# v loaded and cast three pairs later than q and k, the last pieces of w_out moved behind pair 16's casts, and one spread product per unit one step later

## The chip, the cores and the metric

The kernel runs on one core of a Trainium2 chip. The metric is the device time of one execution in microseconds (us); a kernel is run several times and its median is taken. Before the change the median is 483.12 us over 3 runs (481.99 to 483.59).

The engines are TensorE (PE; its weight loads are listed as PEld), VectorE (DVE), ScalarE (ACT), GpSimd (POOL) and SyncE (SP), which here only issues DMAs. Each engine works through its own list of instructions in order and waits on semaphores for the others.

## The reference

```python
# q, k, v: (8, 12, 448, 64); x: (3584, 768), w_in: (768, 2048), w_out: (2048, 768)
scores = scale * np.matmul(q, k.transpose(0, 1, 3, 2))
m = np.max(scores, axis=-1, keepdims=True)
e = np.exp(scores - m)
attn = e / (np.sum(e, axis=-1, keepdims=True) + np.exp(-m) + 1e-09)
attn_out = np.matmul(attn, v)
x = attn_out.transpose(0, 2, 1, 3).reshape(B * S, H * D)
h = x @ w_in
g = h * np.tanh(np.log1p(np.exp(h)))
out = g @ w_out
```

So it is an attention over 8 batches of 12 heads, whose denominator has one extra term, and behind it two dense layers with a Mish between them.

## The kernel before

**Pairs, steps and units.** Two heads make a *pair*: 48 pairs, 6 to a batch. A pair has 4 *steps*, each with up to two blocks of 128 rows of scores. The first 6 pairs are the *head*, a loop of its own (L616). Behind it come *units* of 3 pairs, 12 steps each, n = 0 to 11 (L651, counter u; unit u scores pairs 3u to 3u + 2, so unit 2 has pairs 6 to 8 and unit 4 pairs 12 to 14). Scores are computed three steps ahead of the step whose exponentials run (`scores_ahead`).

**What a step does.** `exps` (ScalarE) takes the exponentials of a step's scores from a PSUM tile `sc` into `en`. `flush_late` then emits the evacuations that earlier steps left in the list `late`. `scores` (TensorE) computes the scores of step n + 3, and VectorE takes their negated maximum (`negm`, L330). Because each engine works in order, the order of these calls is the order on each engine.

**From en to the value product.** `en` has to be transposed to `eT`. Mostly SP issues a DMA transpose for it (`normalise`, L420); pairs 5, 6 and 7 (`BY_PE`) are turned on TensorE in four quarters j (`turn_on_pe`, L432), each followed by an evacuation on VectorE (L435). `av_pair` (L460) multiplies `eT` with `v_bf`; the result goes into `xT` (L475, or L473). For pairs 0 to 11 the division by the denominator is done at this point: `spread_rden` multiplies (TensorE, L391) the reciprocals, split into a high and a low part (`hl`), with an identity, so that each row's reciprocal stands in every row of a PSUM tile, and ScalarE or VectorE copies it to `rb` (L400). From pair 12 on VectorE multiplies `en` itself before the transpose (L412, seven instructions a pair).

**The mo tiles.** There are two PSUM tiles `mo`, handed out by `mo_take` and given back when the evacuation is emitted. The turns, the spreads, the transposes of q and k in the head and in step 4 of unit 2 (`late_tp`), the dummy products that keep TensorE busy (L270) and the two dense layers all use them. When `spread_rden` is called in units 2 and 3, its copy goes to `slow`: it is emitted two steps later on ScalarE, behind that step's exponentials.

**The end of a unit.** After the 12 steps each unit from u = 2 on computes 8 blocks of the first dense layer for a batch (`mm1_mish`, L496, Mish on ScalarE in L502), with the transposes of q and k of the next unit's pairs (L206, evacuated in L242 to L260) and the first scores of the next unit between them. The second dense layer (L549) fills the steps of units from 4 on.

**Loads and casts.** SP's queue, in order, carries the loads of q, k and v (`load_pair`, L128), the DMA transposes and the stores. `ld_pool` has three buffers for each of q, k and v. GpSimd casts q, k and v to bf16 (L179, L180, L186). In the head, pair p + 5 is loaded and pair p + 3 cast in pair p's turn; in a unit, at n = 0, 3 and 6 (`LOAD_AT`), pairs are loaded 4 ahead and cast 3 ahead (`LEAD`). The value product of a pair comes three pairs behind its scores.

**Weights.** GpSimd also issues the DMAs of w_in (12 pieces) and w_out (8 pieces), L162, at the steps in `W_AT`. Where `W_BEHIND` (or the call itself) names a pair, GpSimd first copies two elements of that pair's `eT` (`marks`, L157): it waits there until that transpose has landed. The first four pieces of w_out are the left half of its columns, which unit 4 reads; the last four are the right half, which unit 5 reads first.

Of the kernel before, what the change touches and what calls it, by code (L numbers as in the profile page):

```python
# [19 lines left out]
def kernel(  # L20
# [27 lines left out]
    N_PAIRS = B * HP  # L48
# [59 lines left out]
    def flush_late():  # L108
        while late:
            late.popleft()()  # L110
# [10 lines left out]
    def load_pair(p, names="qkv"):  # L121
        if p >= N_PAIRS:
            return
        b, h0 = p // HP, (p % HP) * 2
        for nm in names:
            src = dict(q=q, k=k, v=v)[nm]
            t = ld_pool.tile([SP_, 2, NT * D], FP32, tag=f"{nm}_f", name=f"{nm}_f")
            nc.sync.dma_start(  # L128
                out=t, in_=src[b, h0 : h0 + 2].rearrange("h (p t) d -> p h (t d)", t=NT)
            )  # L130
            loaded.setdefault(p, {})[nm] = t
# [33 lines left out]
    def cast_pair(p, with_v=True):  # L165
        if p >= N_PAIRS:
            return
        q_f, k_f, v_f = (loaded[p].get(nm) for nm in "qkv")
        q_bf = bf_pool.tile([SP_, NT, 2, D], BF16, tag="q_bf", name="q_bf")
        k_bf = bf_pool.tile([SP_, NT, 2, D], BF16, tag="k_bf", name="k_bf")  # L170
        v_bf = bf_pool.tile([SP_, 2, NT * D], BF16, tag="v_bf", name="v_bf", bufs=12)
        by_t = "p h (t d) -> p t h d"
        q_t, k_t = (t.rearrange(by_t, t=NT) for t in (q_f, k_f))
        if p == 0:
            nc.vector.tensor_copy(out=k_bf, in_=k_t)
            for half in (slice(0, NT // 2), slice(NT // 2, NT)):
                nc.vector.tensor_copy(out=q_bf[:, half], in_=q_t[:, half])
        else:
            nc.gpsimd.tensor_copy(out=q_bf, in_=q_t)  # L179
            nc.gpsimd.tensor_copy(out=k_bf, in_=k_t)  # L180
        casted[p] = (q_bf, k_bf, v_bf)
        if with_v:
            cast_v(p)

    def cast_v(p):
        nc.gpsimd.tensor_copy(out=casted[p][2], in_=loaded.pop(p)["v"])  # L186

    def transpose_pair(p, bank=None):
# [93 lines left out]
    def scores_ahead(limit):  # L282

        while rg["next"] < limit and rg["used"] < len(sc_tiles):
            rg["used"] += 1
            scores(rg["next"])
            rg["next"] += 1
# [301 lines left out]
    LEAD = UNIT_PAIRS + 1  # L589
    LOAD_AT = (0, 3, 6)  # L590
    HEAD = HP

    BY_PE = {HEAD - 1: 1, HEAD: -2, HEAD + 1: 2}
    AV_AT = {0: {1: 3, 5: 4, 8: 5}, 1: {1: 8, 4: 6, 8: 7}}
    RDEN_AT = {0: {0: 3, 2: 4, 6: 5}, 1: {0: 8, 2: 6, 6: 7}, 2: {3: 10, 5: 11}}

    W_AT = ({0: 4, 5: 1}, {1: 2, 3: 1, 5: 1, 7: 1, 9: 1}, {1: 1, 3: 1, 5: 1, 7: 1})
    W_BEHIND = {(0, 0): HEAD - 2, (2, 1): HEAD + 4}
    for p, names in (0, "kq"), (1, "qk"), (0, "v"), (2, "qk"), (1, "v"), (2, "v"):
        load_pair(p, names)  # L600
    keep_busy(8, bank=sc_tiles[0][:, 0, :])
# [14 lines left out]
    for p in range(HEAD):  # L616
        for s in range(STEPS):
            exps(p * STEPS + s)
            if s == 0 and p == 0:
                evac_qk(1, act=True)  # L620
            flush_late()
            if s == 1:
                late.extend(held)
                held.clear()
                flush_late()
            if s == 2:
                evac_qk(p + 2, act=p % 2 == 0)
            scores_ahead(HEAD * STEPS + 3)
            if s == 0:
                transpose_pair(p + 2)  # L630
                if p:
                    denominators(p - 1)
            if s == 1 and p:
                turn_on_pe(p - 1, NT - 1)
            if s == 3 and p == 1:
                load_w(2)
            if s == 2:
                if p >= 3:
                    spread_rden(p - 3)
                cast_pair(p + 3)  # L640
            if s == 3:
                if p >= 3:
                    av_pair(p - 3, hold=True)
                if p + 5 < 10:
                    load_pair(p + 5)
                normalise(p, dma=p not in BY_PE)
            if s < 3:
                keep_busy(2, half=p)
    denominators(HEAD - 1)

    for u in range(UNITS_PER_B, N_UNITS + 2 * UNITS_PER_B):  # L651
        attn = u < N_UNITS
        filler = deque()
        for part in plan.get(u, []):
            filler.extend(mm2_part(*part))
        total, done, acc = sum(w for _, w in filler), 0, 0.0
        p0 = u * UNIT_PAIRS
        if attn and u >= first_mm2:
            av_with.update({p0 + i: p0 + i - UNIT_PAIRS for i in range(UNIT_PAIRS)})
        end = min((u + 1) * UNIT_PAIRS, N_PAIRS) * STEPS  # L660

        for n in range(steps):
            pi, s = divmod(n, STEPS)
            p, idx = p0 + pi, p0 * STEPS + n
            late_tp = u == UNITS_PER_B and n == STEPS
            exps(idx)
            if u == UNITS_PER_B + 1 and n == 0:
                for j in range(2):
                    turn_on_pe(HEAD, j, busy_first=3)
            flush_late()  # L670
            if late_tp:
                transpose_pair(p0 + 2)
                evac_qk(p0 + 2)
            if held and n == 1:
                late.extend(held)
                held.clear()
                flush_late()
            late.extend(slow)
            slow.clear()
            acc += weight[n]  # L680
            want = int(total * acc / sum(weight) + 1e-6)
            while done < want:
                fn, w = filler.popleft()
                fn()
                done += w
            scores_ahead(end)
            if n in LOAD_AT:
                load_pair(p0 + LOAD_AT.index(n) + LEAD)
                cast_pair(p0 + LOAD_AT.index(n) + LEAD - 1)
            for pe, n0 in BY_PE.items():  # L690
                j = n - n0
                first = 2 if pe == HEAD else 0
                if pe // UNIT_PAIRS == u - 1 < first_mm2 - 1 and first <= j < NT:
                    turn_on_pe(pe, j, busy_first=1)
            spread = RDEN_AT.get(u - UNITS_PER_B, {})
            if n in spread:
                on_act = u < first_mm2
                spread_rden(
                    spread[n], copy=nc.scalar.copy if on_act else nc.vector.tensor_copy,
                    behind=slow if on_act else late,  # L700
                )
            early = AV_AT.get(u - UNITS_PER_B)
            if early is not None and n == 7:
                keep_busy(6, bank=mo_free[0])
            if early is not None:
                if n in early:
                    av_pair(early[n], half=p)
            elif s == (2 if pi else 0) and N_PAIRS <= p < N_PAIRS + UNIT_PAIRS:
                av_pair(p - UNIT_PAIRS)
            if u - UNITS_PER_B < len(W_AT):  # L710
                at = (u - UNITS_PER_B, n)
                load_w(W_AT[at[0]].get(n, 0), behind=W_BEHIND.get(at))
        assert done == total

        moe = u < N_UNITS + UNITS_PER_B
        b, w = (u - UNITS_PER_B) // UNITS_PER_B, u % UNITS_PER_B
        nxt = p0 + UNIT_PAIRS
        todo = sorted(range(p0, nxt), key=lambda p: p in BY_PE)
        for f in range(FF_U):
            if moe:  # L720
                mm1_mish(b, w * FF_U + f)
            if u == UNITS_PER_B and f == 3:
                load_w(3, behind=p0 + 2)
            if not attn:
                continue
            if f == 0:
                denominators(p0, UNIT_PAIRS)
                for p in todo if p0 < LATE_DIV else todo[:1]:
                    normalise(p, dma=p not in BY_PE)
            if f == 5 and u == UNITS_PER_B + 1:  # L730
                spread_rden(p0, copy=nc.scalar.copy)
            if f == 4:
                scores_ahead(min(nxt * STEPS + 1, N_PAIRS * STEPS))
            if f in (1, 3, 5):
                transpose_pair(nxt + f // 2, bank=f // 2 % 2)
                evac_qk(nxt + f // 2)
            if f >= FF_U - 2:
                scores_ahead(min(nxt * STEPS + f - FF_U + 4, N_PAIRS * STEPS))
            if f in (3, FF_U - 1) and p0 >= LATE_DIV:
                p = todo[1 + f // (FF_U - 1)]  # L740
                normalise(p, dma=p not in BY_PE)
# [32 lines left out]
```

## Time and profile before

| | before |
|---|---|
| median of 3 runs | 483.12 us |
| the profiled execution | 483.9 us |
| its span, first to last instruction | 482.0 us |
| VectorE busy | 360.3 us (75%) |
| ScalarE busy | 345.3 us (72%) |
| GpSimd busy | 104.3 us (22%) |

How to read the profile: a row of the timeline has start and duration in us, the engine, the line of the kernel, the operation, what it writes and reads (out<-in), how many instructions are merged (x), and in brackets the idle time of the engine before it and what ended it. A row of waits has who waited for whom, the total in us, how often, and the longest. DMAs are issued by SPq and POOL; the time until one lands is told separately. A row of a stretch of time has its bounds, its length, the busy time of each engine with the number of instructions, the granted TensorE clock, the DMA share and GB/s.

### The profile page before, as it was taken

What the parts mean: (1) busy time and instruction counts of PE and PEld (TensorE: products, weight loads), DVE (VectorE), ACT (ScalarE), POOL (GpSimd) and SP (SyncE); (2) the same over time, 40 slices, a digit from 0 to 9 for tenths busy, and PEclk for the clock granted to TensorE, in tenths of its full rate; (3) what the DMA queues carried; (4) which work ended last, traced back from release to release, by engine and by line L of the source; (5) the groups of instructions that cost most, each with busy time, mean ns of one, the idle gap of its engine ahead of it and who ended that gap; (6) DMA issues with size and microseconds to landing.
All of it is one profiled execution on the core that took longest, in us unless ns stands there. A gap on an engine that the chain in (4) does not pass through costs nothing.

```text
span 482.0 us, 9366 instructions
## 1 busy us (share of the span) xinstructions
PE 460.2 (95%) x3291; PEld 257.7 (53%) x3291; DVE 360.3 (75%) x715; ACT 345.3 (72%) x907; POOL 104.3 (22%) x187
## 2 busy tenths in 40 slices
PE   7788899999899999999999999999999999999996
PEld 2344445545555555556555565555555565556563
DVE  5989748669899888889898998888898879421021
ACT  5998868888687869788797968787887978312300
POOL 4633618106022220404040311204040200000000
PEclk9989999999999999999999999999999999999999
DMA  8999999999999979998999999989979695961122
GB/s 238 228 207 220 239 204 216 160 197 248 211 251 228 250 157 211 229 182 224 201 251 164 256 164 219 220 193 227 194 222 197 160 175 121 154 141 34 34 66 67
DMA packets 204976, 91.10 MB, mean 189 GB/s; under 512 B 161792, under 2 KB 201472, under 8 KB 204928
## 3 DMA queue, kind: packets, MB, share of 16 engines
q1 hardware_dynamic: 197408, 84.18, 81.1%
q0 software_dynamic: 7488, 6.29, 9.0%
q8 instruction: 26, 0.43, 0.4%
q14 instruction: 22, 0.18, 0.1%
q10 hardware_dynamic: 32, 0.02, 0.0%
HBM read 45.61 MB, written 11.01 MB: 117 GB/s over the span
## 4 chain that ended last, share of the span: by engine, by line
PE 65%; DVE 7%; ACT 6%; DMA 6%; issue 1%; SPq 0%; DVEq 0%
PE mo L549 23%; PE mo L496 22%; PE sc L309 7%; ACT en L343 6%; PE sc L460 5%; DMA eT<-en 5%; DVE negm L330 4%; PE sc L496 3%; PE sc L206 3%; DVE en L412 1%; DVE xT L473 1%; PE mo L460 1%; DVE o_sb L532 0%; DMA out_dram<-o_sb 0%; DVE qd L252 0%
## 5 line engine op out<-in xcount | busy, mean ns | idle before, releaser
L343 ACT ACTIVATE en<-sc,negm 128x448 bf16<-128x448 f32 x336 | 209.2, 644 | 22.3 <-DVE negm L330 20.6
L330 DVE TENSOR_REDUCE negm<-sc 128x2 f32<-128x896 f32 x192 | 182.8, 970 | 40.6 <-PE sc L309 30.1
L549 PE MATMUL mo<-w_out_sb,gT 128*128 128x384 bf16 (+1 forms) x1024 | 166.7, 306 | 0.4 <-DVE rb L400 0.4
L496 PE MATMUL mo<-xT,w_in_sb 128*128 128x448 bf16 x672 | 142.2, 352 | 1.3 <-DMA w_in_sb<-in_moe_w_in_dram 0.9
L549 PEld LDWEIGHTS <-gT 128*128 128x128 bf16 x1024 | 96.3, 98 | 56.0 <-issue 1.9
L502 ACT ACTIVATE gT<-mo 128x448 bf16<-128x448 f32 x112 | 59.5, 543 | 81.1 <-PE mo L496 80.9
L496 PEld LDWEIGHTS <-w_in_sb 128*128 128x128 bf16 x768 | 72.5, 98 | 65.0 <-issue 3.2
L412 DVE TENSOR_SCALAR en<-en,rden 128x448 bf16<-128x448 bf16 x252 | 74.7, 369 | 0.8
L179 POOL CAST q_bf<-q_f 112x512 bf16<-112x512 f32 x47 | 29.2, 622 | 211.7 <-DMA q_f<-in_q_dram 191.2
L309 PE MATMUL sc<-kT,qd 128*128 128x448 bf16 x252 | 71.6, 354 | 1.8 <-DVE qd L252 1.8
L343 ACT ACTIVATION_READ_ACCUMULATOR en<-sc,negm 128x1 f32 x336 | 72.1, 215 | 0.0
L532 DVE COPY o_sb<-mo 128x384 f32<-128x384 f32 (+1 forms) x64 | 31.9, 498 | 48.3 <-PE mo L549 48.1
L460 PE MATMUL sc<-eT,v_bf 112*64 112x448 bf16 x336 | 39.8, 357 | 1.7 <-DMA eT<-en 0.9
L309 PEld LDWEIGHTS <-qd 128*128 128x128 bf16 x252 | 24.5, 98 | 30.7 <-issue 12.9
L252 DVE TENSOR_SCALAR qd<-sc 64x448 bf16<-64x448 bf16 x72 | 27.8, 386 | 6.0 <-PE sc L206 5.2
L186 POOL CAST v_bf<-v_f 112x512 bf16<-112x512 f32 x48 | 30.0, 625 | 5.7 <-DMA v_f<-in_v_dram 5.4
L180 POOL CAST k_bf<-k_f 112x512 bf16<-112x512 f32 x47 | 29.3, 624 | 7.2 <-DMA k_f<-in_k_dram 5.9
L460 PEld LDWEIGHTS <-v_bf 112*64 112x64 bf16 x384 | 19.8, 109 | 20.5 <-issue 11.8
L260 ACT COPY kT<-sc 128x448 bf16<-128x448 bf16 x39 | 20.8, 533 | 0.6 <-PE sc L206 0.6
L496 PE MATMUL sc<-xT,w_in_sb 128*128 128x448 bf16 x96 | 20.8, 352 | 0.0
L473 DVE CAST xT<-sc 128x448 bf16<-128x448 f32 x33 | 20.3, 615 | 0.0
L206 PEld LDWEIGHTS <-q_bf 112*128 112x128 bf16 x192 | 13.5, 97 | 9.2 <-issue 1.0
(61 smaller groups left out, 281.2 us busy)
## 6 DMA issues: line engine op xcount, KB each, us to landing
k_f<-in_k_dram SPq DMA_DIRECT2D x48, 224.0 KB, 5.0
q_f<-in_q_dram SPq DMA_DIRECT2D x48, 224.0 KB, 4.8
v_f<-in_v_dram SPq DMA_DIRECT2D x48, 224.0 KB, 5.2
w_in_sb<-in_moe_w_in_dram POOLq DMA_DIRECT2D x12, 256.0 KB, 9.5
w_out_sb<-in_moe_w_out_dram POOLq DMA_DIRECT2D x8, 384.0 KB, 10.4
out_dram<-o_sb SPq DMA_DIRECT2D x7, 336.0 KB, 4.0
out_dram<-o_sb SPq DMA_DIRECT2D x8, 288.0 KB, 4.6
out_dram<-o_sb SPq DMA_DIRECT2D x8, 240.0 KB, 3.2
```

The lines of the kernel that those rows point to most:

```text
L179: nc.gpsimd.tensor_copy(out=q_bf, in_=q_t)
L180: nc.gpsimd.tensor_copy(out=k_bf, in_=k_t)
L186: nc.gpsimd.tensor_copy(out=casted[p][2], in_=loaded.pop(p)["v"])
L309: nc.tensor.matmul(sc[:, bk, 0:S], lhsT=qT[:, i].rearrange("d h r -> d (h r)"), rhs=kT, start=True, stop=True,)
L330: half_max[p] = nc.vector.tensor_reduce(out=negm, in_=sc[:, 0 : len(cols), 0:S], axis=AX.X, op=ALU.max, negate=True)
L343: e = nc.scalar.activation(out=st["en"][:, :, c, 0:SP_], in_=sc[:, bk, 0:S].rearrange("q (j c) -> q j c", j=NT), func=AF.Exp, bias=st["neg ...
L412: nc.vector.tensor_scalar(out=en[:, :, i, 0:SP_], in0=en[:, :, i, 0:SP_], scalar1=st["rden"][:, i : i + 1], scalar2=None, op0=ALU.mult,)
L460: mm = nc.tensor.matmul(av[h * 64 : (h + 1) * 64, 0:S], lhsT=v_bf[:, h, j * D : (j + 1) * D], rhs=e_h, start=(j == 0), stop=(j == NT - 1),)
L496: nc.tensor.matmul(h_ps[:, 0:S], lhsT=w_in_sb[:, dm, ff * 128 : (ff + 1) * 128], rhs=xT[b][:, dm, :], start=(dm == 0), stop=(dm == DM_T - 1),)
L502: nc.scalar.activation(out=gT[:, ff, b % 2 * S : b % 2 * S + S], in_=h_ps[:, 0:S], func=AF.Mish)
L532: nc.vector.tensor_copy(out=o_sb[:, cols.start : cols.start + n_dve], in_=st["o"][:, 0:n_dve])
L549: nc.tensor.matmul(st["o"][:, 0:n_cols], lhsT=gT[:, ff, i * 128 : (i + 1) * 128], rhs=w_out_sb[:, ff, cols], start=(ff == 0), stop=(ff == ...
```

## The change

Three things move.

- **v.** In the head, v is loaded for pairs up to 6 and cast for pairs up to 5 only. In a unit, at n = 0, 3 and 6, q and k are loaded 4 pairs ahead and cast 3 pairs ahead as before, v is loaded 1 pair ahead and cast for the pair of that very step. `cast_v` returns for pairs that don't exist.
- **w_out.** In unit 4 the pieces at steps 1, 3, 5 and 7 become pieces at steps 3, 5, 7 and 7, and the marker at step 1, which waited for the transpose of pair 10, goes. Step 3's piece comes behind the casts that step 3 issues, those of pair 16.
- **Spread.** In units 2 and 3, `spread_rden` of the middle one (pairs 4 and 6) is called at step 3 instead of step 2.

```diff
     def cast_v(p):
+        if p >= N_PAIRS:
+            return
         nc.gpsimd.tensor_copy(out=casted[p][2], in_=loaded.pop(p)["v"])
...
-    RDEN_AT = {0: {0: 3, 2: 4, 6: 5}, 1: {0: 8, 2: 6, 6: 7}, 2: {3: 10, 5: 11}}
-
-    W_AT = ({0: 4, 5: 1}, {1: 2, 3: 1, 5: 1, 7: 1, 9: 1}, {1: 1, 3: 1, 5: 1, 7: 1})
-    W_BEHIND = {(0, 0): HEAD - 2, (2, 1): HEAD + 4}
+    RDEN_AT = {0: {0: 3, 3: 4, 6: 5}, 1: {0: 8, 3: 6, 6: 7}, 2: {3: 10, 5: 11}}
+
+    W_AT = ({0: 4, 5: 1}, {1: 2, 3: 1, 5: 1, 7: 1, 9: 1}, {3: 1, 5: 1, 7: 2})
+    W_BEHIND = {(0, 0): HEAD - 2}
...
-                cast_pair(p + 3)
+                cast_pair(p + 3, with_v=p + 3 < HEAD)
...
-                    load_pair(p + 5)
+                    load_pair(p + 5, "qkv" if p + 5 <= HEAD else "qk")
...
-                load_pair(p0 + LOAD_AT.index(n) + LEAD)
-                cast_pair(p0 + LOAD_AT.index(n) + LEAD - 1)
+                at = p0 + LOAD_AT.index(n)
+                load_pair(at + LEAD, "qk")
+                load_pair(at + 1, "v")
+                cast_pair(at + LEAD - 1, with_v=False)
+                cast_v(at)
```

`RDEN_AT` and `W_AT` are indexed by unit - 2; in `RDEN_AT` a step maps to the pair whose reciprocals are spread there.

## The prediction

> **What bounds the kernel now.** I read the page first.
>
> ```profile
> span 482.0 us, 9366 instructions
> PE 460.2 (95%) x3291; PEld 257.7 (53%) x3291; DVE 360.3 (75%) x715; ACT 345.3 (72%) x907; POOL 104.3 (22%) x187
> PE   7788899999899999999999999999999999999996
> DMA  8999999999999979998999999989979695961122
> ```
>
> TensorE is busy 95% of the span, and it is below 9 tenths in the first slices (12 us each) only: whatever this change moves must show before about 125 us. So I asked who TensorE waits for, before and after 122 us, and where.
>
> ```profile
> PE mo L496 <- DMA w_in_sb<-in_moe_w_in_dram: 0.9, 1, 0.9
> PE sc L460 <- DMA eT<-en: 0.9, 1, 0.9
> PE sc L309 <- DVE qd L252: 1.8, 1, 1.8
> PE mo L496 <- DVE xT L473: 0.3, 1, 0.3
> ```
>
> The first two come from the waits up to 122 us, the last two are all there is behind it. So what is won or lost up to 122 us goes through to the end nearly whole. The timeline places the three.
>
> ```profile
> 58.48 1.69 PE L496 MATMUL mo<-xT,w_in_sb 128*128 128x448 bf16 x8 [0.92 <-DMA w_in_sb<-in_moe_w_in_dram]
> 101.31 0.95 PE L460 MATMUL sc<-eT,v_bf 112*64 112x448 bf16 x8 [0.86 <-DMA eT<-en]
> 122.05 0.55 PE L309 MATMUL sc<-kT,qd 128*128 128x448 bf16 x2 [1.75 <-DVE qd L252]
> ```
>
> They are the first w_in product (at the end of unit 2, whose twelve steps belong to pairs 6 to 8; the third piece of w_in is late), the value product of pair 9 (in unit 4, pairs 12 to 14; its transpose is late) and the first scores for unit 5, behind unit 4's normalisation. Together 3.53 us: that is the prize, and none of it is in the steady part.
>
> **v later.** Three v loads (pairs 7, 8, 9) and three v casts leave the head; they come back in the last attention units, where the DMA row has its first 6s and 5s in a row with 9s. TensorE's order of work is unchanged by this part. What does a load cost? At the start, with nothing else on the DMA engines, GpSimd's casts each begin on the landing of their tile; the first and the last of seven in a row:
>
> ```profile
> 8.70 0.62 POOL L179 CAST q_bf<-q_f 112x512 bf16<-112x512 f32 x1 [0.16 <-DMA q_f<-in_q_dram]
> 13.38 0.62 POOL L186 CAST v_bf<-v_f 112x512 bf16<-112x512 f32 x1 [0.17 <-DMA v_f<-in_v_dram]
> 30.00:101.00 71.00, 65.08 (x608) 35.61 (x606) 51.55 (x86) 57.82 (x155) 27.85 (x53) 1.00 1.16 205
> ```
>
> From 8.70 to 13.38 are six steps: 0.78 us a load, 2.3 us for three. The third row is a stretch of time; its last two numbers are the DMA share and GB/s. A share of 1.16 over 71 us is a backlog without a hole, so I take it that all later landings come 2.3 us earlier. The third w_in piece then lands near 56.1, pair 9's transpose near 99.0 instead of 101.3; both waits lose their cause (-0.92 and -0.86) as far as TensorE is not itself later. The three casts (1.9 us of GpSimd) were off the path. At the other end v of pairs 45 to 47 is cast a unit ahead of its product; with the free DMA there I put that at 0, and at 0.78 us a load if a store or a transpose were to wait behind one.
>
> **Spread product one step later.** TensorE does the same 16 small products, but the two PSUM banks `mo` change places. In unit 2, step 4 takes a bank for the transposes of pair 8. Before, that was the bank which the copy of spread 4 (ScalarE) had just freed. Now the spread is one step younger, holds its bank until step 5, and the transposes must take the bank of the third turn of pair 5, behind its evacuation; the fourth turn must then take the same bank again, behind the evacuations of q and k.
>
> ```profile
> 49.06 1.08 DVE L330 TENSOR_REDUCE negm<-sc 128x2 f32<-128x896 f32 x1
> 49.20 0.35 PE L270 MATMUL mo<-busy 128*128 128x448 bf16 x1 [0.41 <-DVE eT L435]
> 49.77 0.36 PE L206 MATMUL mo<-ident,q_bf 112*128 112x112 bf16 x4
> 50.06 0.61 DVE L435 COPY eT<-mo 112x896 bf16<-112x896 bf16 x1
> 50.59 0.38 DVE L242 TENSOR_SCALAR qd<-mo 128x448 bf16<-128x448 bf16 x1
> 51.19 0.61 DVE L330 TENSOR_REDUCE negm<-sc 128x1 f32<-128x448 f32 x1
> 51.72 0.61 DVE L435 COPY eT<-mo 112x896 bf16<-112x896 bf16 x1
> 66.03 0.36 PE L206 MATMUL sc<-ident,q_bf 112*128 112x112 bf16 x4
> 66.70 0.39 DVE L242 TENSOR_SCALAR qd<-sc 128x448 bf16<-128x448 bf16 x1 [0.61 <-PE sc L206]
> 71.03 0.55 PE L432 MATMUL mo<-ident,en 128*112 128x128 bf16 x7
> 71.62 0.62 DVE L435 COPY eT<-mo 112x896 bf16<-112x896 bf16 x1 [0.28 <-PE mo L432]
> ```
>
> VectorE runs here without idle, so a hole in it is paid. The copy at 50.06 frees the bank when the next operation starts, 50.59. TensorE resumes 0.14 behind that (49.06 to 49.20): transposes at 50.73 instead of 49.77. The q evacuation follows 0.67 behind its transposes (66.03 to 66.70): 51.40 instead of 50.59. Evacuating q and k takes 0.60 (50.59 to 51.19), so the bank is free at 52.00; 0.14 later one dummy product of 0.18 (49.20 to 49.38), then the turn, and its copy 0.59 behind (71.03 to 71.62): 52.91 instead of 51.72. Unit 2 is 1.2 us later. The next reduces, the exponentials and the 6 dummy products in front of the w_in product follow in order, so TensorE comes to that product 1.2 later, where it waited 0.92 before: the w_in wait is spent, and 0.3 is left over.
>
> In unit 3 the third turn of pair 7 now takes the second turn's bank instead of the one that spread 6 freed.
>
> ```profile
> 79.28 0.61 DVE L435 COPY eT<-mo 112x896 bf16<-112x896 bf16 x1
> 79.40 0.36 PE L270 MATMUL mo<-busy 128*128 128x448 bf16 x1
> ```
>
> That copy frees its bank at 79.82; TensorE goes on at 79.96 instead of 79.40, and the value product of pair 6 right behind: +0.55, with VectorE waiting for it. Bounds for both together: 0, if VectorE has slack that the rows hide, and 1.75. I take the 1.75 (+1.2 and +0.55), since the path is followed row by row.
>
> **w_out behind pair 16's casts.** The marker, which waited for pair 10's transpose, is gone, and the one w_out issue behind it moves from in front of pair 16's casts to behind pair 17's: four issues instead of three now stand among the casts of pairs 16 to 18, which is all that was queued behind the marker on GpSimd.
>
> ```profile
> 104.35 0.18 POOL L157 COPY marks<-eT 1x2 bf16<-1x2 bf16 x1 [13.78 <-DMA eT<-en]
> 104.58 0.79 POOL L162 DMA_DIRECT2D w_out_sb<-in_moe_w_out_dram x1
> 106.62 0.68 SPq L128 DMA_DIRECT2D q_f<-in_q_dram x1
> 112.49 0.61 POOL L179 CAST q_bf<-q_f 112x512 bf16<-112x512 f32 x1 [7.12 <-DMA q_f<-in_q_dram]
> 118.19 0.74 POOL L162 DMA_DIRECT2D w_out_sb<-in_moe_w_out_dram x1
> 120.05 0.61 POOL L186 CAST v_bf<-v_f 112x512 bf16<-112x512 f32 x1
> DMA to landing us min/median/max: 6.4/7.1/7.6
> 127.00 3.43 PE L549 MATMUL mo<-w_out_sb,gT 128*128 128x192 bf16 x28
> q0 software_dynamic: 509, 0.38, 73.4%
> 116.31 4.99 DVE L412 TENSOR_SCALAR en<-en,rden 128x448 bf16<-128x448 bf16 x7
> 122.84 1.81 DVE L412 TENSOR_SCALAR en<-en,rden 128x448 bf16<-128x448 bf16 x7
> ```
>
> The last two rows are the same work: seven multiplies take 1.81 us alone and 4.99 beside GpSimd's casts, which end at 120.66. This is the 1.75 us wait. The q0 row is the 4 us from 107 to 111: GpSimd's own queue, one w_out piece, took 73% of them, 2.9 us, while q of pair 16 waited to land. Now: q is issued 2.3 us earlier (104.3), without that piece lands 2.3 + 2.9 us earlier at best (107.3) and 2.3 at worst (110.2). The chain from cast 16 to the end of cast 18 was 8.2 us (112.49 to 120.66) with three issues, with four 8.9: it ends between 116.2 and 119.1. The multiplies start at 116.3 as before (the terms so far cancel). Before, they ended 0.6 behind the last cast (121.2 and 120.66), and the two q evacuations took 0.8 more; the same behind a chain that ends at 117.6, the middle, is 119.0, and TensorE, ready at 120.3 (122.05 less 1.75), does not wait: -1.75. A chain that ends at 119.1 leaves 0.2 of it; one that does not move gains 0. The pieces themselves, issued by 117 and landing in 6.4 to 7.6 us (the row of the three from 114 to 119), are there by 125; unit 5, which reads them, begins at 127.0 less the gain: 0.
>
> GpSimd's issue at 118.19, amid those multiplies, took 0.74, the lone one at 104.58 took 0.79. [...]
>
> **The sum** on the profiled execution (483.9 us, span 482.0): +1.2 - 0.92 + 0.55 - 0.86 - 1.75 = -1.8, hence 482.1. That execution is 0.8 above the median of the runs shown, 483.12, so for the median I say 481.3.
>
> **Rivals.** (1) *The bank rotation costs nothing*: the 0.41 us wait at 49.20 is also a bank wait and goes away, but the unbroken VectorE rows speak against. Then -0.92 - 0.86 - 1.75 = -3.5: 479.6. (2) *The change doesn't reach the collision*: loads of pairs 17 and 18 now compete with two w_out pieces, the casts stay beside the multiplies. Then the terms before cancel and nothing is added: 483.1; for it speaks that cast 18 needs the last landings, against it that q of 16 alone gains over 2 us. (3) *Slower*: w_out takes the DMA ahead of everything, as from 107 to 111. Four pieces of 2.9 us from about 112 end at 123.6; three loads (2.3) and pair 12's transpose, issued behind them on SP's queue, follow.
>
> ```profile
> 130.36 0.95 PE L460 MATMUL sc<-eT,v_bf 112*64 112x448 bf16 x8
> DMA to landing us min/median/max: 7.3/7.3/7.3
> ```
>
> The first is its reader, due near 128.6 now; the second is that transpose's time to land. 123.6 + 2.3 + 7.3 = 133.2 would be a wait of 4.6, with the -1.8 +2.8 net: 485.9. It decides from a landing past 128.6, and makes the kernel slower from 130.4. Against it: the transpose need not start only then. [...]
>
> **How the numbers follow.** Forecast 0.50, rival 1 0.17, rival 2 0.23, rival 3 0.10. 0.3% (1.45 us, 481.7) is about what a measurement of this kernel can tell from no change. Faster by more: three quarters of the forecast, all of rival 1, little of 2: 0.58. Slower by more: nearly all of rival 3, 0.10. Within: 0.32. The forecast's own range is 480.6 to 482.0 (0.2 of collision, 0.5 of rotation either way); to leave out no more than 2 in 10 it must reach rivals 1 and 2: 479.4 to 483.4.
>
> **What would show it.** No w_in wait at the first w_in product, but holes of some 0.8 and 0.4 us on VectorE in front of the q evacuation and the last turn's copy of unit 2; no wait for eT at pair 9's value product; q of pair 16 cast before 110; unit 4's first seven multiplies under 3 us and no wait of 1.75 behind them. Wrong: casts still beside the multiplies, a new wait for eT at pair 12, or TensorE waiting in the last two units for v.

## The result, and the profile after

The changed kernel takes 481.81 us (median of 22 runs, 480.42 to 482.62) beside 482.73 of the kernel before (22 runs, 481.29 to 485.35): a ratio of 0.9973, 95% interval 0.9960 to 0.9986. Run again with other experiments it was 0.9984, 0.9970 to 0.9998. So it is a little faster: by 0.8 to 1.3 us by the ratios, by 0.92 and 0.63 us by the two pairs of medians (482.78 and 482.15 the second time); 481.3 was forecast.

In the code and the profile after, every line of the main loop stands two further down: L498 is the first dense layer, L551 the second, L462 the value product, L414 the seven multiplies. The head of the page, and behind it three rows from the view of TensorE's waits up to 125 us (total in us, how often, the longest):

```profile
span 478.9 us, 9363 instructions
PE 460.5 (96%) x3291; PEld 257.7 (54%) x3291; DVE 358.5 (75%) x715; ACT 344.8 (72%) x907; POOL 103.6 (22%) x186
```

```profile
PE mo L393 <- DVE eT L437: 1.9, 5, 0.6
...
PE sc L462 <- ACT en L345: 0.9, 2, 0.6
...
PE mo L208 <- DVE eT L437: 0.8, 1, 0.8
```

The three rows that were the prize (w_in, eT at pair 9, qd L252) are gone. Waits for `eT` L437 are waits for an `mo` bank. Three of the five in the first row lie in the head and are there with the earlier spread too (b1, e2); the other two, 0.35 each at 48.45 and 77.43, and the 0.8 of the third row come with the later spread. Of the 0.9 for ScalarE at the value product, 0.3 was there before; 0.62 is new. The timeline of the changed kernel has them where the prediction looked:

```profile
48.45 0.70 PE L393 MATMUL mo<-ident,hl 128*64 128x128 bf16 x16 [0.35 <-DVE eT L437]
49.98 0.36 PE L208 MATMUL mo<-ident,q_bf 112*128 112x112 bf16 x4 [0.82 <-DVE eT L437]
50.57 0.39 DVE L244 TENSOR_SCALAR qd<-mo 128x448 bf16<-128x448 bf16 x1 [0.65 <-PE mo L208]
52.09 0.62 DVE L437 COPY eT<-mo 112x896 bf16<-112x896 bf16 x1 [0.30 <-PE mo L434]
57.02 2.44 PE L498 MATMUL mo<-xT,w_in_sb 128*128 128x448 bf16 x12
78.96 0.35 PE L272 MATMUL mo<-busy 128*128 128x448 bf16 x1 [0.63 <-DVE eT L437]
100.61 0.95 PE L462 MATMUL sc<-eT,v_bf 112*64 112x448 bf16 x8 [0.62 <-ACT en L345]
107.63 0.61 POOL L179 CAST q_bf<-q_f 112x512 bf16<-112x512 f32 x1 [17.54 <-DMA q_f<-in_q_dram]
115.78 0.62 POOL L188 CAST v_bf<-v_f 112x512 bf16<-112x512 f32 x1
116.25 1.81 DVE L414 TENSOR_SCALAR en<-en,rden 128x448 bf16<-128x448 bf16 x7
119.42 0.54 PE L311 MATMUL sc<-kT,qd 128*128 128x448 bf16 x2
124.36 1.81 PE L551 MATMUL mo<-w_out_sb,gT 128*128 128x192 bf16 x18
```

Read from the top: TensorE waits 0.82 for a bank, which leaves VectorE idle for 0.65 and, a turn later, 0.30; the first w_in product runs 12 in a row with no wait inside; unit 3 has its bank wait; pair 9's product no longer waits for `eT` but for ScalarE; the casts of pairs 16 to 18 end at 116.40, the seven multiplies take 1.81 instead of 4.99, and the scores behind them start without a wait.

To compare executions whose heads differ, I count from the start of the first turn of unit 2. "Start of unit 5" is the start of the 65th w_out product, 1.3 us behind the row at 124.36: unit 5's first 16 still read the left half of w_out, the 65th is the first to read the right half.

| start, us | before | after | from unit 2's first turn |
|---|---|---|---|
| unit 2's first turn (L432, L434) | 45.45 | 44.71 | |
| first w_in product | 56.64 | 57.02 | 11.19, 12.32 |
| fifth, the first to read the third piece | 58.48 | 57.79 | 13.04, 13.09 |
| last w_in products of unit 2 | 68.91 | 67.92 | 23.46, 23.21 |
| first w_in product of unit 3 | 85.76 | 85.31 | 40.32, 40.60 |
| value product of pair 9 | 101.31 | 100.61 | 55.87, 55.90 |
| start of unit 5 | 128.31 | 125.68 | 82.87, 80.98 |
| end of the last product | 477.38 | 474.72 | 431.93, 430.02 |
| span | 482.04 | 478.91 | |

The two profiled spans differ by 3.13: 0.74 ahead of unit 2, 1.89 in units 2 to 4, 0.03 behind them, and 0.47 behind the last product. The prediction's sum is about the second part, the 1.89.

### The profile page after: what moved, and what is told of

Same layout as the page of the kernel before. It is cut to its first block, busy times and chain, and to the rows that moved or that the text cites. A ratio compares the mean times of both kernels' runs of the same rounds, so it can differ in the third digit from the quotient of the medians.

```text
span 478.9 us, 9363 instructions
## 1 busy us (share of the span) xinstructions
PE 460.5 (96%) x3291; PEld 257.7 (54%) x3291; DVE 358.5 (75%) x715; ACT 344.8 (72%) x907; POOL 103.6 (22%) x186
## 4 chain that ended last, share of the span: by engine, by line
PE 70%; ACT 7%; DVE 6%; issue 1%; DMA 0%; SPq 0%; DVEq 0%
PE mo L498 25%; PE mo L551 23%; PE sc L311 8%; ACT en L345 6%; PE sc L462 6%; DVE negm L332 4%; PE sc L498 4%; PE sc L208 3%; DVE xT L475 1%; PE mo L462 1%; DVE eT L437 0%; DMA out_dram<-o_sb 0%; PE mo L272 0%; DVE o_sb L534 0%; DVE xT L477 0%
## 5 line engine op out<-in xcount | busy, mean ns | idle before, releaser
L551 PE MATMUL mo<-w_out_sb,gT 128*128 128x384 bf16 (+1 forms) x1024 | 166.7, 307 | 0.4 <-DVE rb L402 0.4
L498 PE MATMUL mo<-xT,w_in_sb 128*128 128x448 bf16 x672 | 141.9, 353 | 0.3 <-DVE xT L475 0.3
L551 PEld LDWEIGHTS <-gT 128*128 128x128 bf16 x1024 | 96.3, 98 | 56.0 <-issue 1.9
L498 PEld LDWEIGHTS <-w_in_sb 128*128 128x128 bf16 x768 | 72.7, 98 | 63.4 <-issue 3.2
L414 DVE TENSOR_SCALAR en<-en,rden 128x448 bf16<-128x448 bf16 x252 | 72.2, 359 | 0.8
L345 ACT ACTIVATION_READ_ACCUMULATOR en<-sc,negm 128x1 f32 x336 | 71.0, 211 | 0.0
L462 PE MATMUL sc<-eT,v_bf 112*64 112x448 bf16 x336 | 39.8, 357 | 1.4 <-ACT en L345 0.9
L462 PEld LDWEIGHTS <-v_bf 112*64 112x64 bf16 x384 | 20.0, 109 | 20.0 <-issue 11.4
L498 PE MATMUL sc<-xT,w_in_sb 128*128 128x448 bf16 x96 | 20.8, 353 | 0.0
## 6 DMA issues: line engine op xcount, KB each, us to landing
w_out_sb<-in_moe_w_out_dram POOLq DMA_DIRECT2D x8, 384.0 KB, 10.9
```

Source lines behind the costliest of these rows:

```text
L345: e = nc.scalar.activation(out=st["en"][:, :, c, 0:SP_], in_=sc[:, bk, 0:S].rearrange("q (j c) -> q j c", j=NT), func=AF.Exp, bias=st["neg ...
L414: nc.vector.tensor_scalar(out=en[:, :, i, 0:SP_], in0=en[:, :, i, 0:SP_], scalar1=st["rden"][:, i : i + 1], scalar2=None, op0=ALU.mult,)
L462: mm = nc.tensor.matmul(av[h * 64 : (h + 1) * 64, 0:S], lhsT=v_bf[:, h, j * D : (j + 1) * D], rhs=e_h, start=(j == 0), stop=(j == NT - 1),)
L498: nc.tensor.matmul(h_ps[:, 0:S], lhsT=w_in_sb[:, dm, ff * 128 : (ff + 1) * 128], rhs=xT[b][:, dm, :], start=(dm == 0), stop=(dm == DM_T - 1),)
L551: nc.tensor.matmul(st["o"][:, 0:n_cols], lhsT=gT[:, ff, i * 128 : (i + 1) * 128], rhs=w_out_sb[:, ff, cols], start=(ff == 0), stop=(ff == ...
```

## The experiments

Each run's ratio is to the kernel before, run beside it on the same chip. "Unit 5" is its start counted from unit 2's first turn, in the run's one profile; the next three columns are from its timeline.

| run | what it is | ratio, 95% interval | last of the casts ends | seven multiplies | wait behind | unit 5 |
|---|---|---|---|---|---|---|
| before | | 1 | 120.66 | 4.99 | 1.75 | 82.87 |
| b1 | before, again | one run, 482.23 us | 118.83 | 3.48 | 0.95 | 81.29 |
| after | all three parts | 0.9973, 0.9960 to 0.9986 | 116.40 | 1.81 | 0 | 80.98 |
| a1 | after, again | 0.9984, 0.9970 to 0.9998 | 114.09 | 1.81 | 0 | 82.25 |
| e1 | v and w_out | 0.9954, 0.9939 to 0.9968 | 115.42 | 3.09 | 0 | 79.31 |
| e2 | v | 0.9944, 0.9925 to 0.9963 | 114.93 | 1.81 | 0 | 79.32 |
| e8 | v, again | 0.9950, 0.9939 to 0.9962 | 117.85 | 3.93 | 0.90 | 80.58 |
| e3 | spread | 1.0001, 0.9987 to 1.0015 | 118.21 | 3.33 | 0 | 82.24 |
| e4 | w_out | 0.9971, 0.9956 to 0.9987 | 118.08 | 3.47 | 0.28 | 81.25 |
| e9 | v and spread | 0.9987, 0.9975 to 0.9999 | 115.02 | 1.81 | 0 | 82.30 |
| e5 | after, pair 8's transposes at step 5 | 0.9968, 0.9952 to 0.9983 | 115.80 | 2.16 | 0 | 80.80 |
| e6 | v, with three spare loads | 1.0010, 0.9993 to 1.0028 | 119.45 | 4.79 | 1.13 | 82.61 |
| e7 | after, six spare casts | 0.9992, 0.9977 to 1.0007 | 117.78 | 2.94 | 0 | 80.97 |
| e10 | after, eleven spare casts | 1.0002, 0.9993 to 1.0011 | 122.19 | 4.47 | 0.81 | 81.96 |

**The three parts one by one** (e1 to e4).

e1: the changed kernel with `RDEN_AT` as before.

```diff
-    RDEN_AT = {0: {0: 3, 3: 4, 6: 5}, 1: {0: 8, 3: 6, 6: 7}, 2: {3: 10, 5: 11}}
+    RDEN_AT = {0: {0: 3, 2: 4, 6: 5}, 1: {0: 8, 2: 6, 6: 7}, 2: {3: 10, 5: 11}}
```

> The changed kernel with the middle spread product back at step 2 of units 2 and 3 (v and w_out stay changed). Rotation theory: the two holes on VectorE in unit 2 (0.65 and 0.30 in the changed kernel) and those in unit 3 go; counted from the first dummy product of unit 2's turns, the first w_in product starts 1.1 us earlier than in the changed kernel, and no w_in wait comes back; unit 3's w_in product another 0.5 earlier. Against the kernel before: -3.0 to -3.5 us, ratio 0.993 to 0.994. Rival (the rotation is free, or the later spread is itself a gain): the same start or later, ratio 0.997 or above.

e2: the kernel before with the v lines of the change alone (`cast_v`, `load_pair`, `cast_pair`).

> The kernel before with v later alone. Backlog theory: the third w_in piece and pair 9's transpose land about 2.3 us or more earlier, both waits (0.92, 0.86) vanish; q of pair 16 is issued 2 us earlier but the w_out piece behind the marker still stands in front of it, so casts and multiplies of unit 4 still overlap in part: -1.8 to -2.3 us, ratio 0.995 to 0.9965. Rival (the transfers are hidden or the DMA has holes): landings move less than 1 us and the ratio is 0.998 to 1.0.

e3: the kernel before with the new `RDEN_AT` alone.

> The kernel before with the spread product one step later alone. Rotation theory: unit 2 loses 1.1 us on VectorE, of which the w_in wait (0.92) hides most; unit 3 loses 0.5, which the wait for pair 9's transpose (0.86) hides; the wait behind unit 4's multiplies stays: 0 to +0.4 us, ratio 1.000 to 1.001. Rival (the later spread is the gain): 0.998 or below.

e4: the kernel before with the new `W_AT` and `W_BEHIND` alone.

> The kernel before with the last w_out pieces behind pair 16's casts alone, without the marker. Theory: without the w_out piece of 2.9 us of DMA in front of it, q of pair 16 lands near 109.5 instead of 112.4, the casts end near 118.4, the seven multiplies of unit 4 take 2.5 to 3.5 us and the wait behind them (1.75) shrinks to 0.3 or less: -1.4 to -1.7 us, ratio 0.9965 to 0.997. Rival (only v's relief lets the casts escape, four issues lengthen the chain): the wait stays at 1.5 or more, ratio 0.999 to 1.001.

v alone gives the whole gain and more: 0.9944, and unit 5 is 1.66 earlier than in the changed kernel. All that TensorE waits for in e2 from 50 to 125 us, and the multiplies with the scores behind them:

```profile
PE sc L325 <- ACT en L345: 1.0, 1, 1.0
PE sc L462 <- ACT en L345: 0.9, 2, 0.6
PE mo L272 <- DVE eT L437: 0.4, 1, 0.4
PE mo L551 <- DVE rb L402: 0.4, 1, 0.4
PE sc L317 <- DVE xT L477: 0.3, 1, 0.3
```

```profile
115.34 1.81 DVE L414 TENSOR_SCALAR en<-en,rden 128x448 bf16<-128x448 bf16 x7
118.64 0.54 PE L311 MATMUL sc<-kT,qd 128*128 128x448 bf16 x2
```

No wait for w_in, for pair 9's transpose or for `qd` is left. The spread put back (e1) gives the same 1.67, the price of the spread in this trace; the ratio of 0.9954 falls short of the 0.993 to 0.994 expected. Alone (e3) the spread costs nothing in the ratio, as expected if the w_in wait hides it; e3's one profile has a dip of the clock there (below) and can't show this. w_out alone (e4) gains as the changed kernel does, in spite of its own profiled run, the slowest of its twelve (483.07 us beside a median of 480.99). There rival 3 is to be seen, in TensorE's waits from 125 us on and in the timeline of e4:

```profile
PE sc L460 <- DVE negm L330: 1.0, 1, 1.0
PE sc L460 <- DMA eT<-en: 0.7, 1, 0.7
```

```profile
119.96 0.55 PE L309 MATMUL sc<-kT,qd 128*128 128x448 bf16 x2 [0.28 <-DVE qd L252]
129.01 0.95 PE L460 MATMUL sc<-eT,v_bf 112*64 112x448 bf16 x8 [0.68 <-DMA eT<-en]
```

Pair 12's transpose, issued at 119.26, lands at 128.97, 9.7 us later, beside w_out pieces that land until 125.91; the two waits are new. The first row names VectorE, but pair 13's transpose landed at 134.88, 0.13 ahead of the product that waited (135.01), so it is most likely a late transpose too. e4's end is 1.8 us later against unit 5 (the last product ends 350.87 behind unit 5, 349.06 before). So the mechanism of rival 3 exists, at a landing of 129 and not 133, and only while v is not moved: in the changed kernel the pieces are issued earlier and no wait stands behind 125 us but the 0.3 at L498 that was there before.

**The kernel before once more** (b1: an unchanged copy).

> The kernel before, profiled once more, to see which of the numbers read from one execution repeat. Theory: the order of work decides, so the w_in wait (0.9), pair 9's eT wait (0.9) and the 1.8 behind unit 4's multiplies come back within 0.3 us each, and only the place of the granted-clock dips changes. Rival: the backlog of the DMA engines differs between executions by some 3 us, so one of the three waits differs by more than 0.5 us and casts of pairs 16 to 18 end more than 1 us away from 120.66.

From its timeline (lines one further down):

```profile
63.58 0.55 PE L497 MATMUL mo<-xT,w_in_sb 128*128 128x448 bf16 x2 [0.70 <-DMA w_in_sb<-in_moe_w_in_dram]
100.54 0.95 PE L461 MATMUL sc<-eT,v_bf 112*64 112x448 bf16 x8 [0.62 <-ACT en L344]
116.22 3.48 DVE L413 TENSOR_SCALAR en<-en,rden 128x448 bf16<-128x448 bf16 x7
116.31 0.74 POOL L163 DMA_DIRECT2D w_out_sb<-in_moe_w_out_dram  x1
120.46 0.55 PE L310 MATMUL sc<-kT,qd 128*128 128x448 bf16 x2 [0.95 <-DVE qd L253]
```

The rival won. The same program waits for another piece of w_in (the sixth, 0.70), not for pair 9's `eT` at all, and 0.95 instead of 1.75 behind the multiplies; unit 5 is 1.58 earlier. The transfers that TensorE waits for came 1.5 to 1.8 us earlier in this execution (third w_in piece 56.62 instead of 58.44, pair 16's casts from 111.01 instead of 112.49). A prize read from one profile is one draw: 3.53 us in the first, 1.65 and the ScalarE wait in the second.

**Is the bank the reason in unit 2?** (e5)

```diff
-            late_tp = u == UNITS_PER_B and n == STEPS
+            late_tp = u == UNITS_PER_B and n == STEPS + 1
```

> The changed kernel, but the transposes of pair 8 in unit 2 are issued at step 5 instead of step 4, when the later spread has given its bank back. Bank theory: the holes of 0.65 and 0.30 on VectorE in front of the q evacuation and the last turn's copy of unit 2 go, the first w_in product comes 0.6 to 1.1 us earlier against the start of unit 2, at the cost of up to 0.5 in front of the first scores of pair 8; 0.9975 to 0.9995 of the changed kernel, 0.995 to 0.997 of the kernel before. Rival (the bank is not the reason, the later spread delays by its own place on TensorE): the holes stay or move with the transposes, the product stays at 12.3, and the ratio to the kernel before stays at 0.9973.

VectorE in unit 2 of e5:

```profile
50.50 0.62 DVE L437 COPY eT<-mo 112x896 bf16<-112x896 bf16 x1 [0.30 <-PE mo L434]
51.04 0.38 DVE L244 TENSOR_SCALAR qd<-mo 128x448 bf16<-128x448 bf16 x1
52.18 1.09 DVE L332 TENSOR_REDUCE negm<-sc 128x2 f32<-128x896 f32 x1 [0.46 <-PE sc L320]
```

The bank reading holds: moved away from the crowded step, the transposes no longer leave a hole. But the gain does not come: now the turn waits for the bank (0.30), and the first scores of pair 8 wait for their `kT` (0.46). The first w_in product is at 12.15, 0.17 better than 12.32. Three users of two banks leave a hole in both orders tried; only the old place of the spread is without one.

**What v later does: the loads or the casts?** (e6: e2, and in the head three loads of a v pair into a tile that nobody reads)

```diff
-                    load_pair(p + 5)
+                    load_pair(p + 5, "qkv" if p + 5 <= HEAD else "qk")
+                    if p + 5 > HEAD:
+                        h0 = (p + 5) % HP * 2
+                        nc.sync.dma_start(out=spare,
+                            in_=v[1, h0 : h0 + 2].rearrange("h (p t) d -> p h (t d)", t=NT))
```

> The kernel before with v later alone, and three spare loads of a v pair into a tile that nobody reads, in the head, where the loads of v for pairs 7 to 9 stood: the DMA work up to there is as before, the casts are as with v later. Backlog theory: the w_in wait (some 0.9) and pair 9's eT wait come back and casts of pairs 16 to 18 end 2 us later than with v alone (114.9), so that part of the collision returns: 0.997 to 1.000 of the kernel before. Rival (it is the three casts on GpSimd and the place of the later loads that help): the landings stay early and the ratio stays at 0.9944.

```profile
58.40 1.69 PE L499 MATMUL mo<-xT,w_in_sb 128*128 128x448 bf16 x8 [1.80 <-DMA w_in_sb<-in_moe_w_in_dram]
100.72 0.95 PE L463 MATMUL sc<-eT,v_bf 112*64 112x448 bf16 x8 [0.62 <-ACT en L346]
115.28 4.79 DVE L415 TENSOR_SCALAR en<-en,rden 128x448 bf16<-128x448 bf16 x7
120.82 0.55 PE L312 MATMUL sc<-kT,qd 128*128 128x448 bf16 x2 [1.13 <-DVE qd L255]
```

Three loads in the head bring back the w_in wait, now 1.80, the slow multiplies and the wait behind them, and the whole gain is gone (1.0010). So it is the loads, through what queues behind them on the DMA engines; the three casts that e6 still leaves out of the head are worth nothing that the ratio shows. The landings of the third w_in piece, counted from unit 2's first turn, agree: 8.6 to 11.0 us in all nine profiles with v moved and no spare loads, 11.2 to 13.9 in the five others, e6 the latest. Pair 9's `eT` wait alone did not come back. (e6 also has 10 buffers for `v_bf` instead of 12, e7 and e10 have 9; no cast of v in them waits for anything but its load.)

**Do the casts slow the multiplies?** (e7 and e10: the changed kernel with casts of a tile of zeros on GpSimd at step 8 of unit 4; they stand between the casts of pairs 17 and 18, so pair 18's are pushed back too)

```diff
                 load_w(W_AT[at[0]].get(n, 0), behind=W_BEHIND.get(at))
+                if at == (2, 8):
+                    for _ in range(6):          # 11 in e10
+                        nc.gpsimd.tensor_copy(out=spare_b, in_=spare_f)
```

> The changed kernel with six spare casts of 112x512 on GpSimd behind pair 18's, written to a tile that nobody reads, so that GpSimd casts for some 3.7 us more while unit 4's first seven multiplies run. Collision theory: the seven multiplies take 4 us or more instead of 1.81, TensorE waits 1 to 2.2 us for qd behind them, ratio to the kernel before 1.000 to 1.002 (0.9973 plus 1.3 to 2.2 us). Rival (the slow multiplies come from the DMA traffic or from the landing of eT, not from the casts): the multiplies stay under 2.5 us and the ratio stays at 0.9973.

> The changed kernel with eleven spare casts of 112x512 on GpSimd (six in e7_spare_casts), issued between the casts of pair 17 and those of pair 18, so that casts run beside unit 4's first seven multiplies to their end. Collision theory: each us of casting beside the multiplies costs them some 0.7 us (before: 4.35 us beside, 3.18 longer), the seven take 4 to 5 us, they end behind the last cast, TensorE waits 1 us or more for qd, unit 5 at 82 us or later from the start of unit 2, ratio 0.9995 to 1.004. Rival (the landing transfers slow the multiplies, which in e7_spare_casts took 2.94 us): the seven stay under 3.2 us, no wait, ratio as the changed kernel's.

From the timeline of e10 (L417 is the seven multiplies):

```profile
113.07 7.41 POOL L723 CAST spare_b<-spare_f 112x512 bf16<-112x512 f32 x11
116.13 4.47 DVE L417 TENSOR_SCALAR en<-en,rden 128x448 bf16<-128x448 bf16 x7
121.36 0.55 PE L314 MATMUL sc<-kT,qd 128*128 128x448 bf16 x2 [0.81 <-DVE qd L257]
```

In e7 the casts of that execution came some 2.5 us earlier than in the profile after (first at 105.14), so only 2.08 us of casting lay beside the multiplies: 2.94 us, no wait, less than the 4 or more expected. Its ratio, 0.9992, can't be told from the changed kernel's 0.9984. e10 settles it: with casts beside them to the end the multiplies take 4.47, the wait is back at 0.81 (1 or more was expected), and the ratio is 1.0002, 0.67 us above the changed kernel run beside it (a1). In the trace of e10 the multiplies from the second on start 0.68 us apart, as the spare casts beside them do: one multiply for each cast, where alone they follow each other in 0.25. The stretch in which GpSimd's casts, and the issues between them, lie beside the multiplies, and what these take beyond 1.81, go together over all runs: 4.35 and 3.18 before, 4.47 and 2.66 in e10, 3.31 and 2.12 in e8, 2.61 and 1.67 in b1, 1.97 and 1.52 in e3, 0.81 and 0.35 in e5, 0.15 and 0 after. Multiplies that take up to some 1.5 us longer cost TensorE nothing (e3: 3.33 us, no wait); beyond it TensorE waits (3.47 and 0.28 in e4, 3.48 and 0.95 in b1).

**The best version, and the last combination** (a1 and e8: copies of the changed kernel and of e2; e9: e2 with the new `RDEN_AT`)

> The changed kernel once more, as the common measure for the other three runs of this call. Theory: its median is 0.996 to 0.9986 of the kernel before again; against the start of unit 2 the first w_in product comes at 12.3 us and unit 5 at 81.0, within 0.2, since no transfer is late any more. Rival: a late transfer (the w_in piece, a transpose or the casts) returns in this execution as the collision differed between the two looks at the kernel before, and unit 5 comes over 0.5 us later.

> The kernel before with v later alone, once more, as the candidate that beats both kernels. Theory: 0.993 to 0.9963 of the kernel before, 1 to 1.7 us under the changed kernel run beside it, unit 5 at 79.3 us from the start of unit 2. Rival (its first six runs were lucky in their transfers): ratio above 0.9965, no difference to the changed kernel.

> v later and the later spread, without the move of w_out. Theory (w_out's move adds nothing once v is out of the head): unit 5 at 81.0 us from the start of unit 2 as in the changed kernel, ratio 0.996 to 0.9985, the same as the changed kernel within 0.0015. Rival (w_out's move is needed behind the later spread): casts of pairs 16 to 18 end beside the multiplies, these take over 2.5 us, and the ratio is 0.999 or more.

v alone beats both kernels again: 0.9950 beside 0.9984 of the changed kernel, the intervals 0.9939 to 0.9962 and 0.9970 to 0.9998 apart. Its profile shows the collision back all the same (3.93 us, 0.90 of wait): the casts came 2.9 us later than in e2, from the same program, so a gain there depends on the execution. With w_out moved as well, none of the profiles without spare work has that wait (after, a1, e1, e5); of those with v alone or with the spread, one of three has (e8, not e2 and e9). e9, v and spread without w_out, stands with the changed kernel (0.9987 and 0.9984; 0.996 to 0.9985 was expected): w_out's move adds nothing that the median shows once v is moved. Not tried is spread and w_out without v.

a1 and e9 start unit 5 1.3 us later than expected, at 82.25 and 82.30, with no late transfer. The cause is the granted clock; the view of stretches of time for a1, whose third number from the end is that clock, shows it:

```profile
48.50:51.90 3.40, 1.81 (x31) 1.39 (x29) 2.76 (x7) 3.11 (x9) 3.17 (x6) 1.00 0.92 183
```

```profile
51.90:55.30 3.40, 3.34 (x20) 1.59 (x19) 2.20 (x4) 1.05 (x3) 1.84 (x3) 0.50 1.14 255
55.30:58.00 2.70, 2.70 (x30) 1.30 (x28) 2.53 (x3) 2.41 (x8) 0.00 (x0) 1.00 1.18 242
```

and the same place in e8, which has the spread where it was:

```profile
48.00:51.40 3.40, 2.90 (x34) 2.00 (x34) 3.40 (x8) 3.10 (x10) 3.40 (x6) 1.00 0.95 232
```

Behind 3.4 us in which TensorE was busy for 1.81, the clock is halved for the next 3.4; with the earlier spread it is busy for 2.90 there and nothing happens. The holes of the later spread lie in that stretch, and the price is 1.27 us (a1's first w_in product is at 13.59, after's at 12.32). It struck in e3, e9 and a1 of the seven profiles with the later spread, and in none of the seven with the earlier one. In the profile after, the same holes are cut in two by the grid of 3.41 us on which the dips start (last section): TensorE is busy for 2.12 in the step from 49.16 to 52.57 (12 steps behind its dip at 8.21), and no dip follows. That the holes bring it on is likely from this, but no run was made to show it.

## Why the prediction was right, step by step

The forecast for the median, 481.3, met 481.81, and the sum for units 2 to 4, -1.8, met -1.89. That both fit so well has luck in it. Between the medians the kernel gained 0.92 us, half of the 1.8; the forecast started from 483.12, the median of three runs, where 22 give 482.73. The -1.89 compares a long execution of the kernel before (483.9 us) with a short one of the changed kernel (480.78, beside a median of 481.81). And the terms fit less well than their sum:

| term | forecast | measured, from the table of starts |
|---|---|---|
| bank rotation in unit 2 | +1.2 | +1.13 (12.32 less 11.19) |
| third piece of w_in | -0.92 | -1.07 (from the first to the fifth product: 0.77 less 1.84) |
| rest of unit 2 | 0 | -0.30 (between fifth and last products) |
| bank rotation in unit 3 | +0.55 | +0.53 (+0.28 less -0.25) |
| pair 9's transpose | -0.86 | -0.25 (+0.03 less +0.28) |
| collision in unit 4 | -1.75 | -1.92 (-1.89 less +0.03) |

The -0.30 in the rest of unit 2 is another late piece, the sixth of w_in: in the kernel before it landed at 64.06, amid the six products at 63.07, which took 1.59 instead of 1.30.

- *v later relieves the DMA engines*: right, and the cause of the gain (e2, e6). The forecast of 2.3 us was too small if anything here: the third piece landed at 53.79 instead of 58.44, but executions of one program differ by 1.5 to 3 us themselves. Most of it is an earlier issue (46.62 instead of 50.27): GpSimd's marker in front of that piece waits for pair 4's transpose, which landed at 46.44 instead of 50.09.
- *The banks*: right in kind and size in both units, with holes of 0.65 and 0.30 where 0.8 and 0.4 were worked out; rival 1 (no cost) falls with e1. Not seen was its second price, the halved clock. On the median the spread costs 1.8 us without w_out's move (0.9987 less 0.9950 of 482.78, e9 and e8) and 0.9 with it (0.9973 less 0.9954, after and e1, whose intervals overlap).
- *Pair 9's transpose*: the step that failed is the price of a removed wait, -0.86. The transpose did land early (96.12 instead of 101.27), but the product then waited 0.62 for ScalarE. It does so, for 0.62, in all thirteen other profiles, b1 among them. The profile before had the reason, unread:

```profile
98.39 1.28 ACT L343 ACT_TABLE_LOAD   x1
99.68 0.64 ACT L343 ACTIVATE en<-sc,negm 128x448 bf16<-128x448 f32 x1
100.31 0.63 ACT L343 ACTIVATE en<-sc,negm 128x448 bf16<-128x448 f32 x1
```

  Behind a table load of 1.28 us ScalarE's first two exponentials of unit 4 end at 100.94, 0.37 before the product's start at 101.31. In the profile after the second of them is

```profile
99.84 0.62 ACT L345 ACTIVATE en<-sc,negm 128x448 bf16<-128x448 f32 x1
```

  and ends at 100.46, 0.15 before the product's 100.61. So of the 0.86 no more than 0.37 - 0.15 = 0.22 was to be had. A removed wait is worth the distance to the next thing due, not its length.
- *The collision*: right, by the row of 1.81 beside 4.99, and e10 makes it again. q of pair 16 was cast at 107.63 (forecast 107.3 to 110.2) and the casts ended at 116.40 (116.2 to 119.1). That w_out's move was needed for it was not right: v alone does it in e2. In e8 it does not: the wait of 0.90 is half of the 1.75 but no less than b1's 0.95. Rival 2 falls for the changed kernel, but has a point for v alone.
- *GpSimd's issue beside the multiplies*: in b1 the one behind their start took 0.74 (at 116.31, multiplies from 116.22), as the prediction's row had it (0.74, and 0.79 alone); this trace again shows no wait.
- *Rival 3*: not in the changed kernel, but in e4, with 1.8 us instead of 4.6. The transpose landed 3.1 us behind the last piece and 2.4 us later than the 7.3 of before; the rival had loads and a full 7.3 behind the pieces. In e4 SP's queue moved 6 packets from 119.4 to 122 us, behind the issue, and GpSimd's 705; from 122 to 126 it was 1170 and 205. So packets of SP's queue moved before the last piece had landed (125.91).
- *The w_out pieces are there when unit 5 begins*: right, with more room than the prediction's 127.0 gave, since the right half is first read 1.3 us behind that row (128.31 before).
- *v at the end costs nothing*: right; unit 5 to the last product takes 349.04, before 349.06.

Outside the prediction: the 0.74 ahead of unit 2 is no effect of the change (the head of a1 is at 45.36, of b1 at 45.44; the clock's dips there lie otherwise in each execution). The 0.47 behind the last product is one, unforeseen: span less last product is 4.66 before and in b1 and 4.67 in e3, 4.96 in e6, 4.35 in e2, e8 and e9, and 4.18 to 4.20 in all with w_out's move (after, a1, e1, e4, e5, e7, e10). What in the programs makes the last store land earlier stays open.

So of 3.13 us between the two profiles 2.4 belong to the change; the profile before was a bad draw (unit 5 at 82.87, 81.29 in b1) and the profile after a good one (80.98, 82.25 in a1), and the runs together show 0.6 to 1.3.

## What to carry to other kernels

Before a wait is counted as a prize, look up in the same trace what would release the instruction next; and profile the kernel before twice, since a wait for a transfer in a backlog is a draw (pair 9's was 0.86 here in the first profile and none in the second). Of a change in several parts each has to run alone: here one part gives the gain, one pays part of it back, and one adds nothing once the first is in. Here moving loads that are needed late out of a saturated stretch paid at the transfers behind it, and a small product that held one of two banks one step longer cost time in both units where it did so (1.13 and 0.53 us).

## What the runs showed of the hardware

- *The granted clock falls in the middle of work.* The dips, to 0.50 of full speed, start on a grid of about 3.41 us whose phase differs between executions (9.76 and 26.83 in the profile before: 5 steps of 3.41; 8.21 and 21.86 in the profile after: 4; 10.9 and 51.9 in a1: 12). In a1 a step with TensorE busy for 1.81 of 3.4 us was followed by one at half clock, though no single gap in it was over 0.83 us. Busy time alone doesn't decide: e5 has a step with 1.86 of 3.41 us (48.94 to 52.35) and no dip behind it, and where the grid of e6 has the w_in wait, TensorE is busy for 1.70 of 3.41 us, and no dip follows:

```profile
54.90:58.31 3.41, 1.70 (x12) 0.56 (x10) 1.72 (x4) 3.39 (x10) 2.24 (x5) 1.00 1.19 232
```

- *One program's transfers differ by 1.5 to 3 us between executions*: pair 16's first cast is at 106.76 in e2 and at 109.92 in e8, at 112.49 in the profile before and at 111.01 in b1.
- *GpSimd's casts beside VectorE's multiplies cost these 0.4 to 0.8 us for each us* (0.35 for 0.81 in e5, 3.33 less 1.81 for 1.97 in e3).
